# Tokens' rows scattered into expert order, in place of a table of slots

## The chip, the cores and the metric

The kernel runs on one core of one Trainium2 chip. The metric is the device time of one execution in microseconds: the median of several runs. Before the change it is 4458.95 us (three runs, 4456.1 to 4466.6).

## The reference

Three layers, one after the other, on 8 batches of 3072 tokens with 256 columns, in float32:

```python
# 1. spectral layer, for each batch
X = np.fft.rfft(x, axis=1)                                   # over the 3072 tokens
Yr = Xr @ w_r - Xi @ w_i + b_r;  Yi = Xr @ w_i + Xi @ w_r + b_i
Yr = sign(Yr) * max(|Yr| - 0.01, 0)                          # the same for Yi
y = irfft(Yr + 1j * Yi, n=3072, axis=1).reshape(24576, 256)
# 2. mixture of 8 experts, the best one for each token
logits = normalized(y) @ normalized(expert_emb).T / tau
e = argmax(logits);  gate = softmax(logits)[e]
z = gate * (max(y @ w1[e], 0) @ w2[e])                       # 256 -> 1024 -> 256
# 3. dense MLP, 256 -> 2048 -> 256
h = z @ w_in;  out = max(0.01 * h, h) @ w_out                # its weights come in float64
```

## The kernel before

Each product runs as three products of rounded parts (high by high, high by low, low by high), so an eviction from PSUM is a pair: ScalarE copies the high part, VectorE subtracts for the low part (`split_evict`, L165). The order of all work is written out by hand; each engine works in that order, and waits where an operand or a buffer is not ready.

**Spectral layer.** A batch runs through a main stage (`main_step`, L797, steps g = 0 to 25) and a second half (the loop at L868, 37 steps `n2`). The transform over 3072 tokens is one over 96 and one over 32. `s1` (L464) is the first transform over 96; it reads the input tile `xt`, two buffers of 16 rows of 96 tokens, which hold one batch together, loaded in 8 quarters (`load_x`, L355). `mix` (L484) multiplies with the weights, `s2` and `s2i` go over 32 and back. In the second half `swap` (L539) transposes, and `s1i` (L595) makes the last transform over 96: its `ev1` copies the result from PSUM to `yr` (VectorE, L605), `ev2` sums squares (ScalarE, L609), and every second row SP stores two of them to `y1` in DRAM (L613); `yr` has three buffers. In the same steps `s1` already runs for the next batch, whose input tile is thereby read row by row. The last three steps of a second half run together with the first three of the next main stage (`MERGE`).

Beside this, `split_job` (L449) prepares the experts' weights, 128 pieces in all: SP loads one, ScalarE rounds it, GpSimd subtracts, SP stores both parts to DRAM; its tile `hl` has two buffers. It runs in three of four main steps, from step 10 of batch 0 on.

**Routing.** `routing(b)` (L619) gives a list of 22 small steps, most of them on VectorE, that compute each token's expert, gate and slot. Its slots are in regions, one for each expert. The steps are popped from `todo` in the next batch's main stage, one a step, two in every fourth (L815). Then 32 scatters follow (L651), popped from `scat` one a step in that batch's second half (L892): for 96 tokens each, GpSimd writes the token's number, 4 bytes, to its slot in `permd`, the inverse permutation, by an indirect DMA. `block_list` (L692) computes which blocks of 256 slots run, which expert's weights each needs, and gathers the blocks' rows of `permd`, which TensorE turns into the index columns `pidx`. It runs twice: for the 65 blocks surely full after six batches, and for the rest.

**Experts.** `experts` (L193) runs 103 blocks of 256 rows, 8 steps each: `gather_x` fetches the block's rows of `y1` by two indirect DMAs on GpSimd, `trans` transposes them, `mm1` and, a block later, `mm2` multiply; `send` evicts and scatters the rows to `y2` by token (GpSimd, L268). Weights are loaded by SP, addressed by a register. The first blocks run inside the last batch's second half, one step every two, and beside its routing and scatters. Each step also runs one step of `decoder` (L1057), which brings the MLP's weights from float64.

**MLP.** `mlp` (L935) runs 48 tiles of 512 tokens. `load` (L948) fetches a tile of `y2` by a plain transfer on SP, three tiles ahead; before the first one, 24 matmuls on `pw` run (L1041).

Of the kernel before, what the change touches and what calls it, by code (L numbers as in the profile page):

```python
# [1 line left out]

# [8 lines left out]
F32 = mybir.dt.float32  # L11
F32R = mybir.dt.float32r
BF16 = mybir.dt.bfloat16
I32 = mybir.dt.int32
# [14 lines left out]
REG = T // BLK  # L29
NROW = E * REG + E - 1  # L30
# full blocks of the tokens of all batches but two; the rest
# [3 lines left out]
# three runs take turns, with a set of weights each; a run goes through its part of the second list  # L35
# backwards, so that it begins there with the expert that its part of the first ended with
# [3 lines left out]
# a batch's second half: buffers of the swapped rows, steps from the swap to the last transform, and  # L40
# the steps that the next batch's first ones run with
# [17 lines left out]
def constants():  # L59
# [75 lines left out]
    li[:, NA + 1:] = T * np.arange(E)  # L135
# [6 lines left out]
def build(ctx: ExitStack, tc: tile.TileContext, a: dict, out: bass.AP):  # L142
# [6 lines left out]
    permd = dram.tile([NROW * BLK, 1], I32, name="permd")  # L149
    gated = dram.tile([T], F32, name="gated")  # L150
    y1 = dram.tile([T + 1, D], F32, name="y1")
    y2 = dram.tile([T, D], F32, name="y2")
# [9 lines left out]
    pidx = keep.tile([128, 2, NBLK], I32, name="pidx")  # L162
    dummy = keep.tile([1, 1], F32, name="dummy")

# [28 lines left out]
    def experts(st, big, extra):  # L193
        """Yields after each step."""
        def pool(name, bufs):
            return st.enter_context(tc.tile_pool(name=name, bufs=bufs, side="right", reuse_waits="tile"))
        wp, xp, tp, hp, op = pool("ew", 1), pool("ex", 3), pool("et", 2), pool("eh", 10), pool("eo", 4)
        W1, W2 = big
        for s in (1, 2):
            W1.append(wp.tile([128, 4096], F32R, name=f"W1_{s}"))  # L200
            W2.append(wp.tile([128, 4096], F32R, name=f"W2_{s}"))
# [6 lines left out]
        def gather_x(b):  # L208
            if b >= NBLK:
                return  # L210
            i = lidx(b)
            t = xp.tile([128, 2, D], F32R, tag="xg", name="xg")
            for h in range(2):
                nc.gpsimd.indirect_dma_start(
                    out=t[:, h, :].bitcast(F32), out_offset=None, in_=y1[0:TA, :] if b < NA else y1,
                    in_offset=IndirectOffsetOnAxis(ap=pidx[:, h, i:i + 1], axis=0))
            xg[b] = t

# [42 lines left out]
        def send(b, t, p):  # L261
            i = lidx(b)
            o = op.tile([128, D], F32, tag="o", name="eo")
            if t == 0:
                nc.scalar.activation(o, p, AF.Copy)  # L265
            else:
                nc.vector.tensor_copy(o, p)
            ins = nc.gpsimd.indirect_dma_start(  # L268
                out=y2, out_offset=IndirectOffsetOnAxis(ap=pidx[:, t, i:i + 1], axis=0),
                in_=o, in_offset=None, bounds_check=T - 1, oob_is_err=False)  # L270
            nc.gpsimd.memset(dummy, 0.0)
            no_dep(ins, "y2", "every token is written once")

        def finish(b):
            p = O.pop(b)
            for t in range(2):
                send(b, t, p[:, t, :])

        def last(b):
            """The second product of the last block, one half after the other."""  # L280
            w = W2[b % 3].rearrange("p (s f d) -> p s f d", s=2, f=8)
            for t in range(2):
# [7 lines left out]
                send(b, t, p)  # L290

        gather_x(0)
        gather_x(1)
# [4 lines left out]
        for b in range(NBLK):  # L298
            for f in range(8):
# [4 lines left out]
                if f == 2:  # L304
                    gather_x(b + 2)
# [13 lines left out]
    # ------------------------------------------------------------ spectral layer, routing  # L319
    def spectral(big, expert_start):  # L320
        with ExitStack() as st, ExitStack() as mst:
# [50 lines left out]
            def prologue2(wst):  # L372
                # behind the first loads
# [14 lines left out]
            def prologue3():  # L388
                """What a batch's second half needs; a list of small steps."""
# [5 lines left out]
                w = NROW * BLK // 1280  # L395
                pads = {}

                def fill():
                    """Padding entries of the slot table; the row that they point to."""
                    zrow = rp.tile([1, D], F32, tag="lg", name="zrow")  # L400
                    pad = pads[0] = rp.tile([128, w], I32, tag="inc", name="pad")
                    nc.gpsimd.memset(pad, T)
                    nc.gpsimd.memset(zrow, 0.0)
                    nc.sync.dma_start(y1[T:T + 1, :], zrow)
# [8 lines left out]
                def trans():  # L413
                    """The normalized expert embeddings, transposed."""
# [7 lines left out]
                def init():  # L422
# [4 lines left out]
                slots = permd.rearrange("(p q) o -> p (q o)", p=128)  # L427
# [3 lines left out]
                         trans, init, fill]  # L431
                        + [lambda q=q: nc.sync.dma_start(slots[:, w * q:w * q + w], pads[0]) for q in range(10)])

            # the experts' weights, split into their two parts in DRAM
# [146 lines left out]
            def logits3():  # L581
# [8 lines left out]

                return ev

            cur = {}

            def s1i(b, n2):  # L595
                """Returns the two halves of its eviction."""
# [546 lines left out]
```

## Time and profile before

| what | value |
|---|---|
| median of 3 runs | 4458.95 us (4456.1 to 4466.6) |
| profiled execution, its span | 4538.9 us; the trace holds no time around it |
| TensorE busy | 4309.5 us (95%) |
| VectorE, ScalarE, GpSimd busy | 2305.2, 1848.4, 799.5 us |
| mean granted TensorE clock | 0.966 |
| spectral layer with routing | 0 to 1099 us |
| last routing, experts | to 2332 us |
| MLP | to 4538.9 us |
| indirect DMAs: `permd`, `xg`, `y2` | 256, 206, 206 |

The page cuts the span into 40 slices of 113 us. Busy share in tenths, the granted clock of TensorE in tenths, and GB/s moved:

```
PE   9897777887999999999999999999999999999999
PEclk9898878898999999999999999999999999999999
GB/s 175 121 125 91 99 85 109 112 67 122 38 109 114 95 96 94 235 50 118 149 48 19 29 20 29 19 29 19 29 20 29 19 29 19 29 20 29 20 19 15
```

The first ten slices are the spectral layer; from the eleventh on TensorE is busy nearly all the time. Second halves and main stages are cut below at the first `swap` transpose of a batch (L542) and at its fourth `mix` (L492).

### The profile page before, as it was taken

The page shows a single profiled execution, that of the slowest core. Times are in us where ns is not written, and L with a number is a line of the kernel's source. Part 1 is how long each engine was busy: PE and PEld are TensorE (multiplying, and loading weights), DVE is VectorE, ACT ScalarE, POOL GpSimd, SP SyncE. Part 2 cuts the span into 40 slices and gives each one's busy share as a digit, 9 for nine tenths or more (in the row PEclk, how much of TensorE's full clock was granted, in tenths as well). Part 3 has the DMA queues.
Part 4 walks back from the last instruction along what each step waited for, and adds up shares of the span by engine and source line. Part 5 has one row for each costly group of instructions (what it writes and reads, how often), then busy time and mean ns, then how long its engine had stood idle before and what let it go on. Part 6 is the DMA issues. An engine that isn't in the chain of part 4 may idle for free.

```text
span 4538.9 us, 78688 instructions
## 1 busy us (share of the span) xinstructions
PE 4309.5 (95%) x30288; PEld 3982.4 (88%) x30288; DVE 2305.2 (51%) x4836; ACT 1848.4 (41%) x4172; POOL 799.5 (18%) x1298
## 2 busy tenths in 40 slices
PE   9897777887999999999999999999999999999999
PEld 8776666776899999999998999998999999999898
DVE  5665555674345555543344444444444444444453
ACT  4454443443233333333344444444444444444443
POOL 1323334304533333333310000000000000000000
PEclk9898878898999999999999999999999999999999
DMA  6443333326133222613410000000000000000000
GB/s 175 121 125 91 99 85 109 112 67 122 38 109 114 95 96 94 235 50 118 149 48 19 29 20 29 19 29 19 29 20 29 19 29 19 29 20 29 20 19 15
DMA packets 136458, 305.14 MB, mean 67 GB/s; under 512 B 27716, under 2 KB 80444, under 8 KB 131732
## 3 DMA queue, kind: packets, MB, share of 16 engines
q1 hardware_dynamic: 105236, 241.27, 17.1%
q0 software_dynamic: 30848, 58.85, 4.3%
q8 instruction: 239, 3.92, 0.4%
q14 instruction: 135, 1.11, 0.1%
HBM read 542.30 MB, written 111.88 MB: 144 GB/s over the span
## 4 chain that ended last, share of the span: by engine, by line
PE 89%; issue 5%; another core or an unknown queue 3%; DMA 1%; POOL 1%; DVE 1%; ACT 1%; SPq 0%; POOLq 0%; ACTq 0%; DVEq 0%
PE mpH L979 24%; PE mpO L1004 24%; PE pH L242 13%; PE pO L258 13%; PE pu L492 5%; PE py L514 2%; PE ps L470 2%; PE pyo L578 2%; PE pz L530 1%; PE pv L542 1%; PE pT L226 1%; PE mpT L964 1%; PE mpl L1031 0%; POOL permd L655 0%
## 5 line engine op out<-in xcount | busy, mean ns | idle before, releaser
L1004 PE MATMUL mpO<-W,mgh 128*128 128x256 f32 x6016 | 1103.4, 281 | 0.0
L979 PE MATMUL mpH<-mxh,W 128*128 128x512 f32 x3072 | 1087.2, 395 | 0.3 <-ACT mxh L166 0.3
L985 DVE TENSOR_TENSOR mg<-mpH,ms 128x512 f32<-128x512 f32 x768 | 530.8, 691 | 1091.0 <-ACT ms L984 1089.8
L1004 PEld LDWEIGHTS mpO<-W,mgh 128*128 128x128 f32 x6016 | 965.3, 188 | 61.7
L984 ACT ACTIVATE ms<-mpH 128x512 f32<-128x512 f32 x768 | 459.2, 598 | 1234.4 <-PE mpH L979 1231.8
L1004 PE MATMUL mpO<-W,mgl 128*128 128x256 f32 x3008 | 842.0, 280 | 0.0
L242 PE MATMUL pH<-xh,W 128*128 128x256 f32 x3296 | 734.0, 285 | 8.9 <-ACT xh L166 4.8
L246 DVE SCALAR_TENSOR_TENSOR ehl<-pH,ehh 128x256 fp32r<-128x256 f32 x824 | 346.9, 423 | 646.7 <-ACT ehh L245 549.7
L979 PEld LDWEIGHTS mpH<-mxh,W 128*128 128x128 f32 x3072 | 575.1, 187 | 107.4 <-ACT mxh L166 0.5
L258 PE MATMUL pO<-W,ehh 128*128 128x256 f32 x3264 | 632.3, 286 | 4.6 <-issue 2.7
L245 ACT ACTIVATE ehh<-pH 128x256 fp32r<-128x256 f32 x824 | 310.1, 383 | 791.4 <-PE pH L242 763.1
L979 PE MATMUL mpH<-mxl,W 128*128 128x512 f32 x1536 | 605.4, 394 | 0.2 <-DVE mxl L167 0.2
L242 PEld LDWEIGHTS pH<-xh,W 128*128 128x128 f32 x3296 | 576.7, 193 | 12.7 <-issue 5.4
L1004 PEld LDWEIGHTS mpO<-W,mgl 128*128 128x128 f32 x3008 | 565.8, 188 | 0.0
L994 DVE TENSOR_TENSOR mgl<-mg,mgh 128x512 fp32r<-128x512 f32 x768 | 522.6, 680 | 0.0
L258 PEld LDWEIGHTS pO<-W,ehh 128*128 128x128 f32 x3264 | 508.9, 192 | 5.5 <-issue 5.5
L993 ACT ACTIVATE mgh<-mg 128x512 fp32r<-128x512 f32 x768 | 480.2, 625 | 0.0
L242 PE MATMUL pH<-xl,W 128*128 128x256 f32 x1648 | 468.8, 284 | 2.3 <-issue 2.1
L258 PE MATMUL pO<-W,ehl 128*128 128x256 f32 x1632 | 462.9, 284 | 2.1 <-issue 2.1
L268 POOL DMA_INDIRECT y<-eo,pidx x206 | 207.5, 1007 | 730.4 <-ACT eo L265 695.5
L242 PEld LDWEIGHTS pH<-xl,W 128*128 128x128 f32 x1648 | 318.5, 193 | 3.4 <-issue 3.4
L979 PEld LDWEIGHTS mpH<-mxl,W 128*128 128x128 f32 x1536 | 287.9, 187 | 36.7 <-DVE mxl L167 0.5
(192 smaller groups left out, 5520.8 us busy)
## 6 DMA issues: line engine op xcount, KB each, us to landing
W<-w1d SPq DMA_DIRECT2D x101, 2048.0 KB
W<-w2d SPq DMA_DIRECT2D x101, 2048.0 KB
xt<-in_x_dram SPq DMA_DIRECT2D x64, 384.0 KB
y<-yr SPq DMA_DIRECT2D x128, 192.0 KB
mxr<-y SPq DMA_DIRECT2D x47, 512.0 KB
out_dram<-mo SPq DMA_DIRECT2D x47, 512.0 KB
wf<-in_moe_w_dram SPq DMA_DIRECT2D x128, 128.0 KB
w1d<-hl SPq DMA_DIRECT2D x64, 256.0 KB
```

Of the source, the lines that this page charges most:

```text
L242: nc.tensor.matmul(p, l, r, start=(i == 0), stop=(i == 5))
L245: nc.scalar.activation(hh, p, AF.Relu)
L246: nc.vector.scalar_tensor_tensor(hl, p, 0.0, hh, op0=ALU.max, op1=ALU.subtract)
L258: nc.tensor.matmul(O[b][:, t, :], l, r, start=(f == 0 and i == 0 and t == 0), stop=(f == 7 and i == 2 and t == 1))
L268: ins = nc.gpsimd.indirect_dma_start(out=y2, out_offset=IndirectOffsetOnAxis(ap=pidx[:, t, i:i + 1], axis=0), in_=o, in_offset=None, bound ...
L492: nc.tensor.matmul(p, l, r, start=(i == 0), stop=(i == 5))
L979: nc.tensor.matmul(p, l, r, start=(j == 0), stop=(j == 5))
L984: nc.scalar.activation(s, p, AF.Copy, scale=0.01)
L985: nc.vector.tensor_tensor(g, p, s, op=ALU.max)
L993: nc.scalar.activation(gh, g, AF.Copy)
L994: nc.vector.tensor_tensor(gl, g, gh, op=ALU.subtract)
L1004: nc.tensor.matmul(O[i][t // 2][:, t % 2, :], l, r, start=(f == 0 and j == 0 and t % 2 == 0), stop=(f == 15 and j == 2 and t % 2 == 1))
```

## The change

The table of slots goes, and with it `y1`, `y2` and `pidx`. New DRAM tensors: `xs`, the rows in slot order (regions of 97 blocks for each expert, and 7 blocks of padding), `ys`, the experts' results in the order of the blocks, and `slotd`, each token's slot.

- The last transform's rows are not stored to `y1`: they are copied into the next batch's input tile, in the place of the row that `s1` has read (for the last batch into a tile of their own, `y7`).
- When the slots are known, GpSimd scatters these rows of 1 KB to `xs`, two scatters in each main step of the next batch after step 10, and one in each step of its second half until none is left. Only then is the input tile loaded for the batch after: in main steps 21 to 24 and steps 4 to 7 of the second half, a quarter each.
- `todo` is popped three times a main step; weight splitting runs in steps 4 and later of batch 0, and in steps 3 to 13 of the others, two pieces in odd steps.
- `block_list` gathers nothing; it gives the blocks' first rows `wrow`, which SP reads into a register, and the tables `thr`, `off` and `dlt`, by which `places` computes where a token's result lies, in 35 small VectorE steps behind the decoder's. The first list runs a batch earlier.
- A block of the experts is one plain load from `xs` and one plain store to `ys`, both on SP. Behind the last slots of each expert zeros are scattered (`pad`); the padding blocks are written at the start from a tile of zeros.
- The MLP loads a tile by four indirect gathers on GpSimd from `ys`.

Its core:

```diff
-        def gather_x(b):
+        def load_x(b):
             i = lidx(b)
+            r = nc.sync.value_load(wrow[0:1, i:i + 1], min_val=0, max_val=(NROW - 1) * BLK)
             t = xp.tile([128, 2, D], F32R, tag="xg", name="xg")
-            for h in range(2):
-                nc.gpsimd.indirect_dma_start(
-                    out=t[:, h, :].bitcast(F32), out_offset=None, in_=y1[0:TA, :] if b < NA else y1,
-                    in_offset=IndirectOffsetOnAxis(ap=pidx[:, h, i:i + 1], axis=0))
+            nc.sync.dma_start(t.bitcast(F32), xs[bass.ds(r, BLK), :].rearrange("(p h) d -> p h d", h=2))
...
         def finish(b):
             p = O.pop(b)
-            for t in range(2):
-                send(b, t, p[:, t, :])
+            o = op.tile([128, 2, D], F32, tag="o", name="eo")
+            nc.scalar.activation(o[:, 0], p[:, 0], AF.Copy)
+            nc.vector.tensor_copy(o[:, 1], p[:, 1])
+            nc.sync.dma_start(result(b), o)
...
+            def row(b, n2):
+                if b == B - 1:
+                    return y7[0][:N1, n2, :]
+                return xt[b + 1, n2 // 4][:, n2 % 4, :]
...
                 def ev1():
-                    nc.vector.tensor_copy(yr[:, n2 % 2, :], p)
+                    nc.vector.tensor_copy(yr, p)
...
-                    if n2 % 2 == 1:
-                        r0 = b * S
-                        nc.sync.dma_start(
-                            y1[r0:r0 + S, :].rearrange("(p r) d -> p r d", r=N2)[:, n2 - 1:n2 + 1, :],
-                            yr)
...
                 def scatter(n2):
-                    if n2 == 0:
-                        nc.gpsimd.iota(tok, pattern=[[1, N2]], base=b * S, channel_multiplier=N2)
                     nc.gpsimd.memset(dummy, 0.0)
                     ins = nc.gpsimd.indirect_dma_start(
-                        out=permd, out_offset=IndirectOffsetOnAxis(ap=si[:, n2:n2 + 1], axis=0),
-                        in_=tok[:, n2:n2 + 1], in_offset=None)
-                    no_dep(ins, "perm", "every slot is used once")
+                        out=xs, out_offset=IndirectOffsetOnAxis(ap=si[:, n2:n2 + 1], axis=0),
+                        in_=row(b, n2), in_offset=None)
+                    no_dep(ins, "in", "every slot is used once")
...
                 if g >= 3:
-                    for _ in range(2 if last else 1 + (g % 4 == 3)):
+                    for _ in range(3):
                         if todo:
                             todo.pop(0)()
...
-                if g % 4 < 3 and (b or g > 9):
+                if g > 10:
+                    for _ in range(2):
+                        scatter()
+                if g >= 4 if b == 0 else 3 <= g < 14:
                     split_job()
-                if not last and g % 3 == 1 and g // 3 < 8:
-                    load_x(b + 1, g // 3)
+                    if b and g % 2:
+                        split_job()
+                if b == 0 and g % 3 == 1 and g // 3 < 8:
+                    load_x(1, g // 3)
+                if b and g in (21, 22, 23, 24):
+                    refill(b + 1, g - 21)
...
+            nc.gpsimd.dma_start(
+                xs[E * REG * BLK:, :].rearrange("(n p) d -> p n d", p=128),
+                warm.bitcast(F32)[:, None, :].to_broadcast([128, 2 * (E - 1), D]))
...
+                    scatter()
+                    if b and n2 in (4, 5, 6, 7):
+                        refill(b + 1, n2)
...
             def load(i):
-                n = 2 if i == 0 else 4
-                for t in range(0, 4, n):
-                    nc.sync.dma_start(xr[i][:, t:t + n].bitcast(F32), y2v[:, 4 * i + t:4 * i + t + n, :])
+                for t in range(4):
+                    nc.gpsimd.indirect_dma_start(
+                        out=xr[i][:, t].bitcast(F32), out_offset=None, in_=ys,
+                        in_offset=IndirectOffsetOnAxis(ap=slot[:, 4 * i + t:4 * i + t + 1], axis=0))
```

`refill(b, q)` is `load_x` of the spectral layer where there is such a batch; behind the last one it loads the first block's expert weights. In the experts' pools `eh` goes from 10 to 9 buffers and `eo` from 4 of 256 columns to 2 of 512.

## Rows read from the trace of the kernel before

**Rows 1.** Windows, experts and MLP: stretch and us; each engine's busy time; clock, DMA, GB/s.

```profile
1325.00:2335.00 1010.00, 1010.00 (x8494) 1009.36 (x8493) 484.57 (x1261) 338.45 (x876) 351.27 (x508) 1.00 0.33 113
2335.00:4538.90 2203.90, 2199.06 (x14219) 1979.78 (x14217) 1085.16 (x1728) 941.44 (x1728) 0.00 (x0) 1.00 0.07 24
```

**Rows 2.** Windows, second halves of batches 1 to 6: first, last, sum. Engines: PE, PEld, DVE, ACT, POOL.

```profile
194.80:273.80 79.00, 49.38 (x345) 42.47 (x345) 32.70 (x87) 33.08 (x117) 34.36 (x69) 0.74 0.22 51
...
885.40:960.80 75.40, 49.62 (x345) 42.80 (x345) 32.93 (x87) 32.06 (x114) 24.30 (x49) 0.75 0.15 40
sum 467.80, PE 299.26 PEld 262.29 DVE 198.02 ACT 198.29 POOL 195.68; mean PE 49.88 PEld 43.71 DVE 33.00 ACT 33.05 POOL 32.61
```

**Rows 3.** Windows: second half 0, mains 1 and 7, second half 7, last scatters.

```profile
95.50:136.30 40.80, 40.51 (x346) 37.07 (x346) 32.68 (x89) 33.30 (x117) 2.51 (x4) 1.00 0.35 102
136.30:194.80 58.50, 58.10 (x375) 52.18 (x374) 48.10 (x113) 28.40 (x60) 13.03 (x17) 1.00 0.60 173
960.80:1019.70 58.90, 57.37 (x359) 50.62 (x357) 48.92 (x140) 23.54 (x41) 1.41 (x2) 1.00 0.20 77
1019.70:1099.40 79.70, 48.23 (x294) 40.73 (x295) 27.82 (x75) 26.99 (x99) 39.32 (x73) 0.72 0.72 125
1138.00:1253.00 115.00, 105.02 (x809) 100.50 (x809) 34.13 (x80) 29.94 (x80) 64.68 (x111) 0.97 0.18 37
```

**Rows 4.** Timeline of VectorE, batch 1's second half: start, us, instruction, [idle before <-releaser].

```profile
203.67 0.41 DVE L545 TENSOR_TENSOR vl<-pv,vh 96x256 fp32r<-96x256 f32 x1
215.25 0.42 DVE L605 COPY yr<-pyo 96x256 f32<-96x256 f32 x1 [11.17 <-remote]
```

**Rows 5.** Timeline of TensorE in the same stretch.

```profile
205.41 1.01 PE L470 MATMUL ps<-f,xt 96*128 96x96 f32 x4
216.62 0.63 PE L542 MATMUL pv<-ident,Z 128*96 128x128 f32 x2 [10.20 <-issue]
```

**Rows 6.** Timeline of GpSimd in the same stretch; nine more scatters lie between.

```profile
203.60 0.91 POOL L655 DMA_INDIRECT permd<-tok,si  x1 [0.22 <-issue]
...
216.36 0.91 POOL L655 DMA_INDIRECT permd<-tok,si  x1 [0.83 <-DMA permd<-tok,si]
```

**Rows 7.** Waits of the whole run: waiter <- waited for: total us, times, longest.

```profile
DVE yr L605 <- remote: 130.0, 16, 13.1
...
POOL permd L655 <- DMA permd<-tok,si: 42.1, 27, 4.5
```

**Rows 8.** Windows: the start, the loads of constants, plain steps of main stage 0.

```profile
0.00:22.00 22.00, 17.01 (x115) 14.07 (x116) 7.39 (x14) 7.59 (x14) 3.71 (x11) 0.93 0.82 204
20.00:48.00 28.00, 27.00 (x137) 24.03 (x137) 14.83 (x34) 9.93 (x19) 11.14 (x21) 0.78 1.15 302
...
67.90:95.40 27.50, 27.25 (x180) 24.51 (x179) 19.18 (x45) 11.97 (x25) 6.22 (x8) 1.00 0.67 193
```

**Rows 9.** Instructions on tile `hl`: ns min/median/max, first and last start.

```profile
L458 ACT ACTIVATE hl<-wf x128: 400/408/419, 66.1 to 874.5; 128x256 fp32r<-128x256 f32 x128
L459 POOL TENSOR_TENSOR hl<-wf,hl x128: 724/742/904, 66.6 to 875.0; 128x256 fp32r<-128x256 f32 x128
L460 SPq DMA_DIRECT2D w1d<-hl x64: 545/546/1353, 67.5 to 851.9; - x64
```

**Rows 10.** Timeline of ScalarE: a splitting copy that waits for its buffer.

```profile
167.55 0.42 ACT L458 ACTIVATE hl<-wf 128x256 fp32r<-128x256 f32 x1 [0.74 <-DMA w1d<-hl]
```

**Rows 11.** Timeline of SP: the store whose landing that copy awaited.

```profile
164.52 0.55 SPq L460 DMA_DIRECT2D w1d<-hl  x1
```

**Rows 12.** Timeline of GpSimd: the last scatter of the experts.

```profile
2332.61 0.98 POOL L268 DMA_INDIRECT y<-eo,pidx  x1 [1.81 <-DVE eo L267]
```

**Rows 13.** Timeline of SP: the first loads of the MLP.

```profile
2335.08 1.77 SPq L954 DMA_DIRECT2D mxr<-y  x4
```

**Rows 14.** Instructions of line L684, VectorE, in routing: ns min/median/max.

```profile
L684 DVE TENSOR_TENSOR ex<-ex,ob x8: 411/958/965, 176.2 to 1132.7; 96x256 f32<-96x256 f32 x8
```

**Rows 15.** Instructions of line L1092, VectorE, in the experts' stage.

```profile
L1092 DVE TENSOR_TENSOR e<-e,p x32: 412/415/417, 1342.6 to 1986.6; 128x256 f32<-128x256 f32 x32
```

More of the change, by code (lines that the diff above doesn't have):

```diff
@@ L1 @@
 from contextlib import ExitStack
+from itertools import chain
 import numpy as np
@@ L259, in mm2 @@
                                      stop=(f == 7 and i == 2 and t == 1))
[L261 to L272, printed above, removed]
         def finish(b):
             p = O.pop(b)
-            for t in range(2):
-                send(b, t, p[:, t, :])
+            o = op.tile([128, 2, D], F32, tag="o", name="eo")
+            nc.scalar.activation(o[:, 0], p[:, 0], AF.Copy)
+            nc.vector.tensor_copy(o[:, 1], p[:, 1])
+            nc.sync.dma_start(result(b), o)
         def last(b):
             w = W2[b % 3].rearrange("p (s f d) -> p s f d", s=2, f=8)
+            o = op.tile([128, 2, D], F32, tag="o", name="eo")
             for t in range(2):
@@ L430, in prologue3 @@
                          dma(trif, a["tri"]), dma(scan, a["scan"]), dma(eord, a["eord"]), dma(li, a["li"]),
[L431 to L432 removed]
+                         trans, init])
             jobs = []
@@ L690, in routing, with pad, index, scatter @@
                 return steps, sc
+            def pad():
+                zero = rp.tile([128, D], F32, tag="ex", name="zero")
+                zi = rp.tile([128, E, 2], I32, tag="zi", name="zi")
+                co = rp.tile([128, E], F32, tag="co", name="zco")
+                v = nc.vector
+                def index():
+                    v.memset(zero, 0.0)
+                    v.tensor_tensor(co, carry, li[:, NA + 1:], op=ALU.add)
+                    v.tensor_scalar(co, co, li[:, NA:NA + 1], None, op0=ALU.add)
+                    v.tensor_copy(zi[:, :, 0], co)
+                    v.tensor_scalar(zi[:, :, 1], co, 128.0, None, op0=ALU.add)
+                def scatter(e, h):
+                    nc.gpsimd.memset(dummy, 0.0)
+                    ins = nc.gpsimd.indirect_dma_start(
+                        out=xs, out_offset=IndirectOffsetOnAxis(ap=zi[:, e, h:h + 1], axis=0),
+                        in_=zero, in_offset=None)
+                    no_dep(ins, "in", "rows behind the last slot")
+                return [index] + [lambda e=e, h=h: scatter(e, h) for e in range(E) for h in range(2)]
             def block_list(last):
@@ L896, in spectral @@
                         next(ex)
-                assert not scat and not squares
+                assert not squares
                 if last:
@@ L932, in spectral, with places, mlp @@
             return ex
-    def mlp(W):
+    def places(wp, row):
+        slot, s, t = (wp.tile([128, 256], I32, tag=t, name=t + "p").bitcast(F32)[:, :T // 128] for t in "ept")
+        yield lambda: nc.sync.dma_start(slot, slotd.rearrange("(p t) -> p t", p=128))
+        yield lambda: nc.vector.tensor_copy(s, slot)
+        for j in range(2 * E):
+            c = slice(j, j + 1)
+            yield lambda: nc.vector.tensor_scalar(t, slot, thr.rearrange("p e l -> p (e l)")[:, c], dlt[:, c],
+                                                  op0=ALU.is_ge, op1=ALU.mult)
+            yield lambda: nc.vector.tensor_tensor(s, s, t, op=ALU.add)
+        yield lambda: nc.vector.tensor_copy(row, s)
+    def mlp(W, slot):
         with ExitStack() as st:
@@ L1108, in build @@
             W = ml.tile([128, 16384], F32R, name="W")
-            steps = decoder(ml, W)
+            row = ml.tile([128, T // 128], I32, name="row")
+            steps = chain(decoder(ml, W), places(ml, row))
             for _ in ex:
```

155 lines of the change are left out of this document (76 added, 79 removed).

## The prediction

> **What bounds the kernel now.** I cut the span by stage first. In the two long stages at the end, 1325 to 2335 us (experts) and 2335 to 4538.9 us (MLP), TensorE is busy 1010.0 of 1010.0 us and 2199.1 of 2203.9 us at clock 1.00 [rows 1]: nothing that only moves data can shorten them. What can be won or lost lies in the first 1325 us.
>
> There the batches' second halves stand out. Batch 0's takes 40.8 us with TensorE busy 40.5 at clock 1.00; those of batches 1 to 6 run the same 344 to 346 matmul records in 75 to 81 us each, 467.8 us in all, at clocks of 0.70 to 0.76 [rows 2, 3]. Batch 7's, which has expert steps in it, takes 79.7 us at clock 0.72. The main stages between (23 steps of some 2.55 us) are healthy: 58.1 of 58.5 us busy at 1.00 [rows 3].
>
> The difference is the permutation scatter. GpSimd issues one 4-byte-per-row scatter per step, and in a burst they follow at about 1.2 us each. Some 8 us into a burst everything else stops: VectorE finishes at 204.08 and its next row copy starts at 215.25 after 11.17 us idle, for an event that the profile cannot name; TensorE finds 10.20 us idle [rows 4, 5]. GpSimd itself walks on, until it too waits for one of its own scatters to land [rows 6]. Over the run the row copies lose 130.0 us that way and the scatters 42.1 us on their own landings [rows 7]. Batch 0's second half has no scatters and no stall. The 32 scatters of the last batch, spread over 115 us, leave TensorE 105.0 us busy at clock 0.97 [rows 3]. So a dense burst of 4-byte DRAM writes costs a second half 37 us: idle TensorE, and the 1.2 GHz clock level after it.
>
> The profiled span, 4538.9 us, is 80 us above the median of 4458.95. Since the last 3214 us sit on TensorE at full clock, these 80 us must be in the stalls, which the recording lengthens; I sum against 4538.9 and say below why the result stands for the median too.
>
> **The change part by part.**
>
> *Second halves, batches 1 to 6.* The y1 store and its three buffers go; the row copy writes into the input tile of the next batch, whose row TensorE read some five steps earlier. The scatters move to main stages; two of 32 stay. Each should become batch 0's: 467.8 - 6 x 40.8 = 223 us gained [rows 2, 3]. Ends: nothing gained if the stall follows the scatters, 223 if it is theirs alone. I take 223, because a burst of 1 KB rows is a different load: from 20 to 48 us GpSimd's queue and SP's moved 302 GB/s in packets of 0.4 to 4 KB and TensorE was busy 27.0 of 28.0 us [rows 8], and the experts' stage fetches and sends 1 KB rows by indirect transfers with no idle TensorE [rows 1]. What is late next there is the input tile: its second half loads in steps 4 to 7, after the last scatters landed, for a transform at step 12, eight steps or 9 us later; a load of this kind needs 3 to 4 us at the quarter-tile rate of [rows 8] (384 KB at 204 GB/s is 1.9 us, queued up to four deep). Hidden; without that cover some 3 us a batch.
>
> *Second half of batch 7.* Its matmuls are stretched like the others': 48.2 us busy there, and 49.9 in the mean of batches 1 to 6 against 40.5 unstalled [rows 2, 3], so 48.2 x 40.5/49.9 = 39 us. The first expert block now waits in SP's queue for the scatters issued so far, as its rows are addressed by a register; TensorE wants it five steps in. I add 4 us and some slack: 44 us, a gain of 36. Ends: 0 and 40.
>
> *Startup and batch 0.* A padding write of 1792 rows, 1.8 MB, joins the first input loads, when the DMA engines are 0.82 busy at 204 GB/s [rows 8]: 9.0 us if the loads queue behind it, 0 if it slips between. Weight splitting starts at step 4 instead of 10, one job a step. I take +6, range 0 to 13.
>
> *Main stages, batches 1 to 6.* Three things are squeezed. (a) The weight-splitting jobs, 17 a batch over 23 steps, go into steps 3 to 13, three per two steps. A job holds one of two `hl` buffers from ScalarE's copy to its store's landing: 0.41 + 0.74 + 0.55 us [rows 9] and the landing, which the wait at 167.55 puts 2.5 us after its store's issue ended at 165.07 [rows 10, 11]: 4.2 us, so two buffers pass a job each 2.1 us. 17 jobs want 35.7 us, the 11 steps have 28. ScalarE waits in order, with the next `uh` eviction that TensorE needs behind it; by my estimate some 2.5 us of that is absorbed at the two ends, 5 us is not. (b) Routing's 22 steps come three a main step instead of 1.25. VectorE is 0.70 busy in plain steps [rows 8], so 40.8 of main 1's 48.1 us [rows 3] are base and 7 to 8 are routing; squeezed into 8 steps (20.4 us) it wants 22, and it also collides with splitting (below). It shares (a)'s steps, so I count only the larger. (c) From step 11 GpSimd does two scatters a step, 2.4 us of 2.55, and in steps 11 to 13 five splitting ops of 0.74 us wait behind them, with ScalarE's buffers: +3. Together +8 a batch, 48 us; ends 0 and 20 each. After step 13 nothing on GpSimd is waited for until the input tile is refilled.
>
> *Main stage 7.* Four jobs are left and routing is squeezed the same way: +3 (0 to 5).
>
> *Block lists, gather of slots, eh 10 to 9, eo 4 to 2.* The lists lose a gather and gain some small vector steps in the middle of TensorE's full stage; a ninth `hh` frees with the product before it. 35 vector steps for the MLP's places run as extra expert steps. 0, hidden behind the 1010 us of TensorE [rows 1]; without cover 10 us.
>
> *Experts to MLP.* Before: a 0.98 us scatter at 2332.61, landed by 2335.08 when SP loads [rows 12, 13]. Now a store on SP (0.55 + 2.5 as above, so +0.6), and then four gathers at 1.2 us where two loads stood, 3.7 us until the fourth is issued. +4, ends 2 and 7. In the MLP 192 gathers of 1 us lie beside 2204 us.
>
> Sum: 4538.9 - 223 - 36 + 6 + 48 + 3 + 4 = 4341 us. This holds for the median: once the stalls are gone no stretch is left in which the recording could cost 80 us, so the median gains 80 us less, 118 us (2.6%).
>
> **One rule weighed.** Next to splitting, VectorE's two-input multiply of routing takes 958 ns in most batches and 411 at least; next to indirect transfers two-input ops stay at 417 ns at most [rows 14, 15]. The Trainium skill ("SBUF — State Buffer", section "SBUF: two separate sides") says that such a VectorE op and a GpSimd op share one port pair as an exclusive lock, each waiting out the other's whole instruction. The trace agrees for splitting and not for descriptor writing. If indirect transfers also locked it, each of 15 steps in 7 main stages would give VectorE 1.8 + 0.9 = 2.7 us against 2.55, some 20 us.
>
> **Rivals.**
> - *The stall moves with the scatters* (the other side). Were the cause GpSimd's dense issue, whatever is written, the burst of 30 scatters at 1.2 us would stop the main stages 1 to 7 as it stops second halves now. For it: the rate is the same, and the queue is the same. Against: [rows 8], and the experts' 1 KB rows. The change loses as soon as more than two thirds of the median's stall survives, since then what is left of 179 us falls under the 61 us of costs. Wholly moved: 4459 + 61 = 4520 us.
> - *Half the stall survives*, for instance as late landings that hold the input tile: half of the median's 259 - 80 = 179 us, so 4341 + 90 = 4431.
> - *The squeezed main stages cost more*: (a), (b) and (c) add up instead of overlapping, 20 us a batch: 4341 + 72 = 4413. For it: ScalarE, VectorE and GpSimd are all near full in the same steps.
> - *They cost nothing*, as the slack between engines is larger than I think: 4341 - 51 = 4290.
> - *The lock holds for row scatters too*: 4341 + 20 = 4361.
>
> **How the numbers follow.** The forecast 4341, own range 4300 to 4385, has 0.56. The stall moves 0.13; half survives 0.08; main stages cost more 0.15; they cost nothing 0.05 (and a little below); the lock 0.03. The range of 8 in 10 reaches from 4285 to 4425; left out are the first rival and most of the second. A measurement tells 0.2% (9 us) here. Faster takes all cases but the first: 0.85; the same, where losses just balance, 0.02; slower 0.13.
>
> **What would show it.** Right: second halves 1 to 6 near 41 us at clock 1.00; no wait of VectorE's row copy for an unnamed event; scatter bursts from main step 11 with TensorE busy beside them; ScalarE waiting in line L458's successor for stores of `hl` in steps 3 to 13; profiled span and median within some 20 us. Wrong: a main stage of 80 us or more with clock under 0.8, or PE gaps of 10 us inside a burst. A second half of 50 us with gaps at step 12 would say that the refill is late.

## The result, and the profile after

The changed kernel takes 4343.3 us (median of four runs, 4339.2 to 4345.5); the kernel before, run beside it, 4462.8 (4456.1 to 4469.9). The ratio is 0.973, with a 95% interval of 0.9716 to 0.9744: 119.5 us gained, where 118 were forecast. The profiled execution after has a span of 4337.4 us.

The windows of the changed kernel, cut at the same marks as [rows 1 to 3] (stretch, us, then busy time of PE, PEld, DVE, ACT, POOL, and clock, DMA share, GB/s). In order: second halves of batches 0, 1 and 6, with the sum of all seven; main stages 1 and 3, with the sum of 1 to 6; main stage 7 and second half 7.

```profile
96.10:136.90 40.80, 40.55 (x344) 36.99 (x345) 32.49 (x87) 32.30 (x115) 0.73 (x1) 1.00 0.08 24
204.00:244.70 40.70, 40.42 (x344) 36.98 (x345) 32.59 (x87) 32.28 (x114) 4.17 (x9) 1.00 0.21 56
...
750.30:791.10 40.80, 40.51 (x346) 37.04 (x346) 32.66 (x89) 32.35 (x114) 4.08 (x9) 1.00 0.23 55
sum 285.10, PE 283.24 PEld 258.98 DVE 228.26 ACT 226.25 POOL 26.63; mean PE 40.46 PEld 37.00 DVE 32.61 ACT 32.32 POOL 3.80
...
136.90:204.00 67.10, 62.30 (x375) 52.78 (x373) 49.72 (x113) 28.31 (x59) 41.46 (x73) 1.00 0.54 162
...
354.10:423.60 69.50, 63.30 (x376) 52.76 (x374) 49.31 (x113) 29.71 (x60) 41.38 (x73) 1.00 0.53 156
...
sum 409.90, PE 376.93 PEld 317.62 DVE 302.77 ACT 176.81 POOL 248.64; mean PE 62.82 PEld 52.94 DVE 50.46 ACT 29.47 POOL 41.44
...
791.10:852.40 61.30, 57.99 (x355) 50.27 (x354) 47.19 (x111) 25.25 (x47) 33.66 (x64) 1.00 0.36 111
852.40:893.80 41.40, 36.14 (x295) 32.65 (x296) 26.70 (x75) 26.52 (x100) 3.71 (x8) 0.96 0.69 254
```

The stall is gone: a second half with the next batch's transform in it takes 40.7 us at clock 1.00, where [rows 2] show 79.0 and 75.4 at 0.74 and 0.75. The main stages, GpSimd busy in them for 41 us in place of 13, became 6 to 10 us longer; TensorE is idle 5 to 6 us in each, and the rest is in longer busy time.

Behind the spectral layer the stage of the experts, from the last `swap` to the last product, and that of the MLP have to be cut at the same marks in both kernels. Before:

```profile
1099.40:2331.90 1232.50, 1222.52 (x10217) 1217.63 (x10216) 568.80 (x1486) 410.51 (x1068) 453.64 (x674) 1.00 0.31 106
2339.50:4538.90 2199.40, 2195.53 (x14200) 1977.30 (x14200) 1085.11 (x1728) 940.77 (x1727) 0.00 (x0) 1.00 0.07 23
```

After:

```profile
893.80:2106.90 1213.10, 1213.10 (x10216) 1212.78 (x10214) 589.35 (x1529) 418.15 (x1068) 48.76 (x95) 1.00 0.32 113
2118.20:4337.40 2219.20, 2215.79 (x14200) 2004.71 (x14200) 1085.30 (x1728) 940.44 (x1727) 182.06 (x186) 1.00 0.07 23
```

So the whole difference of the two spans, 201.5 us, comes apart like this; it is larger than the 119.5 us of the timed runs because the profiled execution before is 80 us longer than those (see "The median" below). The main stages 1 to 6 of the kernel before run from 58.5 to 61.9 us:

```profile
sum 356.70, PE 350.16 PEld 313.39 DVE 289.20 ACT 177.29 POOL 85.44; mean PE 58.36 PEld 52.23 DVE 48.20 ACT 29.55 POOL 14.24
```

| stretch | before | after | measured | forecast |
|---|---|---|---|---|
| up to main stage 1 | 136.3 | 136.9 | +0.6 | +6 |
| main stages 1 to 6 | 356.7 | 409.9 | +53.2 | +48 |
| second halves 1 to 6 | 467.8 | 244.3 | -223.5 | -223 |
| main stage 7 | 58.9 | 61.3 | +2.4 | +3 |
| second half 7 | 79.7 | 41.4 | -38.3 | -36 |
| experts | 1232.5 | 1213.1 | -19.4 | 0 |
| experts to MLP | 7.6 | 11.3 | +3.7 | +4 |
| MLP | 2199.4 | 2219.2 | +19.8 | 0 |

Two terms of 19 to 20 us were put at nothing, and cancel.

The waits of the changed kernel (total us, times, longest) that answer to [rows 7] and to the forecast of main-stage costs:

```profile
ACT hl L449 <- DMA w2d<-hl: 62.7, 38, 3.3
...
ACT hl L449 <- DMA w1d<-hl: 56.0, 40, 2.8
...
DVE xt L602 <- PE pyo L569: 22.2, 28, 1.4
```

The row copy (now into `xt`) waits for its own product and for nothing unnamed; 130.0 us of [rows 7] are gone. New are the 118.7 us in which ScalarE's splitting copy waits for stores of `hl`. In the kernel before they were 4.9 and 1.1:

```profile
ACT hl L458 <- DMA w1d<-hl: 4.9, 5, 2.8
```

### The profile page after: what moved, and what is told of

Read it like the earlier page. It is cut to its first block, busy times and chain, and to the rows that moved or that the text cites. A ratio compares the mean times of both kernels' runs of the same rounds, so it can differ in the third digit from the quotient of the medians.

```text
span 4337.4 us, 78356 instructions
## 1 busy us (share of the span) xinstructions
PE 4280.0 (99%) x30286; PEld 3960.8 (91%) x30286; DVE 2335.4 (54%) x4880; ACT 1855.3 (43%) x4172; POOL 578.6 (13%) x893
## 4 chain that ended last, share of the span: by engine, by line
PE 83%; issue 7%; POOL 5%; DMA 3%; DVE 1%; ACT 1%; SPq 0%; ACTq 0%; POOLq 0%
PE mpO L1041 25%; PE mpH L1016 25%; PE pO L267 14%; PE pH L251 14%; POOL xs L642 4%; PE pu L483 1%; DMA w2d<-hl 1%; DMA w1d<-hl 1%; POOL hl L450 1%; PE pT L235 1%; PE mpT L1001 1%; PE py L505 1%; PE mpl L1068 1%; PE ps L461 0%; PE pz L521 0%
## 5 line engine op out<-in xcount | busy, mean ns | idle before, releaser
L1041 PE MATMUL mpO<-W,mgh 128*128 128x256 f32 x6016 | 1123.6, 283 | 0.0
L1041 PEld LDWEIGHTS mpO<-W,mgh 128*128 128x128 f32 x6016 | 976.9, 188 | 61.2
L1041 PE MATMUL mpO<-W,mgl 128*128 128x256 f32 x3008 | 853.6, 284 | 0.0
L989 POOL DMA_INDIRECT mxr<-ys,row x192 | 187.9, 979 | 2865.8 <-PE mpT L1001 1772.9
```

Of the source, the lines that this page charges most:

```text
L989: nc.gpsimd.indirect_dma_start(out=xr[i][:, t].bitcast(F32), out_offset=None, in_=ys, in_offset=IndirectOffsetOnAxis(ap=slot[:, 4 * i + t: ...
L1041: nc.tensor.matmul(O[i][t // 2][:, t % 2, :], l, r, start=(f == 0 and j == 0 and t % 2 == 0), stop=(f == 15 and j == 2 and t % 2 == 1))
```

## The experiments

Three groups: what makes the stall, what the squeezed main stages cost, and whether the difference between chips belongs to the kernel. They ran in three sessions on three chips, where the kernel before showed 4557.6, 4454.4 and 4445.0 us (medians of three, seven and three runs).

**No scatters at all.** The kernel before, with its 256 scatters gone. Not in the diff below: as the table of slots then holds padding alone, the blocks gather other rows, the experts' sends drop out, and the MLP reads `y1`.

```diff
...
-                sc = [lambda n=n: scatter(n) for n in range(N2)]
+                sc = [lambda: None for n in range(N2)]
...
```

> The kernel before without its permutation scatters (left out: the 256 scatters of 4 bytes; the blocks take other rows, the sends of rows drop out by their bound or land elsewhere, the MLP reads y1). All else, the y1 stores of the second halves too, stays. Theory (the burst of 4-byte writes stops the engines): second halves 1 to 7 become like batch 0's, 41 us at clock 1.00, no wait of the row copy for an unnamed event; time about 4463 - 179 = 4284 us, and the profiled span within 20 us of it, as nothing is left that the recording lengthens. Rival (the second half stalls by itself, through the y1 stores and row copies that share it): second halves stay over 70 us, time above 4430 us. In between: the difference to 4284 is what the stores cost.

Measured: 4251.6 us, beside 4557.6 for the kernel before, ratio 0.933 (0.930 to 0.936). The sums of its second halves 1 to 6 and of its main stages 1 to 6:

```profile
sum 244.30, PE 242.80 PEld 222.09 DVE 195.77 ACT 198.25 POOL 12.12; mean PE 40.47 PEld 37.01 DVE 32.63 ACT 33.04 POOL 2.02
...
sum 352.00, PE 349.64 PEld 313.62 DVE 289.60 ACT 177.29 POOL 77.54; mean PE 58.27 PEld 52.27 DVE 48.27 ACT 29.55 POOL 12.92
```

With the y1 stores still there the second halves are 244.3 us, to a tenth what the change reached: the stores cost nothing, the scatters all of it. The time came out 32 us lower than expected. The 179 us of the expectation counted the second halves alone; the profiles of the kernel before and of this one also differ by 19.1 us in the experts' stage, where the last batch's scatters run, and by 4.7 in main stages 1 to 6. The window of that stage, TensorE busy throughout, where the kernel before took 1232.5 us:

```profile
830.10:2043.50 1213.40, 1213.40 (x10217) 1213.03 (x10216) 565.90 (x1486) 409.42 (x1068) 421.61 (x609) 1.00 0.32 88
```

On this chip all that the scatters cost is 4557.6 - 4251.6 = 306 us.

**The scatters alone moved.** The kernel before, its 4-byte scatters in the next main stage.

```diff
-                    for _ in range(2 if last else 1 + (g % 4 == 3)):
+                    for _ in range(3):
...
+                if g > 10:
+                    for _ in range(2):
+                        if scat:
+                            scat.pop(0)()
...
```

> The kernel before with one thing of the change alone: its 4-byte scatters go into the next batch's main stage, two in each step after step 10, with routing three steps at a time ahead of them. Theory (the 4-byte burst stalls whatever stands beside it): the stall moves with the scatters, main stages 1 to 6 grow to 85 to 100 us with gaps of TensorE near 10 us and clock under 0.85, second halves shrink to 41; time within 50 us of the kernel before, 4415 to 4515. Rival (the stall needs the scatters and the y1 stores of the second half together): no gap in the main stages, over 100 us faster, about 4320.

Measured: 4483.2 us, ratio 0.984 (0.979 to 0.989). Windows of its main stage and second half 3, and TensorE's longest gap there (start, us, instruction, idle before it):

```profile
388.60:475.00 86.40, 67.21 (x375) 57.70 (x373) 47.83 (x113) 29.73 (x62) 40.45 (x74) 0.88 0.65 122
...
475.00:521.70 46.70, 43.95 (x344) 40.06 (x345) 32.81 (x87) 33.20 (x117) 7.00 (x13) 0.93 0.34 85
```

```profile
467.42 0.58 PE L514 MATMUL py<-uh,g2h 128*128 128x256 f32 x1 [8.54 <-ACT uh L166]
```

The stall went with the scatters: the main stage 86.4 us at clock 0.88 with a gap of 8.5 us, the second half, in which GpSimd still has 7.0 us of work, 46.7 where 41 was expected. 232 us above the kernel without scatters remain of 306, so moving them is worth 74 us in this kernel, more than the 50 I gave as a limit. Most of the stall stays as long as 4 bytes are written; the next runs change that alone.

**The changed kernel, writing 4 bytes of each row.** First into a dense table as before, which the diff below shows; then at the row's own place, 1 KB apart. In both the experts' blocks load other rows.

```diff
-                        out=xs, out_offset=IndirectOffsetOnAxis(ap=si[:, n2:n2 + 1], axis=0),
-                        in_=row(b, n2), in_offset=None)
+                        out=permd, out_offset=IndirectOffsetOnAxis(ap=si[:, n2:n2 + 1], axis=0),
+                        in_=row(b, n2)[:, 0:1], in_offset=None)
...
```

> The changed kernel with its 256 row scatters writing 4 bytes of each row into a dense table, as the kernel before did (left out: the other 1020 bytes; the experts' blocks take other rows). Same issue, same steps, same indices. Theory (what is written decides): gaps near 10 us come into main stages 1 to 7, their clock falls under 0.85, each grows by 20 to 37 us; time 4343 + 7 x 24 = 4510 us (range 4460 to 4600), profiled span above the median by 30 us or more. Rival (GpSimd's issue at that rate, or the second half, made the stall): no change, 4335 to 4350.

> The changed kernel with its row scatters writing 4 bytes of each row, at the row's own place in xs, so 1 KB apart (left out: the rest of each row; the experts' blocks take other rows). If the size of a write decides: as with the dense table, 4510 us (4460 to 4600) with gaps near 10 us in the main stages. If it is neighbours in the same dense table that decide (several writes into one stretch of memory): no gaps, 4335 to 4350 us.

Measured: 4613.4 us (ratio 1.012, 1.009 to 1.016) and 4602.5 (1.010, 1.007 to 1.013). Main stage 1, its second half and main stage 3 of the kernel with 4 bytes at 1 KB:

```profile
137.50:234.10 96.60, 65.91 (x375) 54.94 (x373) 49.33 (x113) 28.20 (x59) 44.91 (x81) 0.86 0.37 103
234.10:274.90 40.80, 40.51 (x346) 37.07 (x346) 32.69 (x89) 32.38 (x114) 0.00 (x0) 1.00 0.01 2
412.30:511.10 98.80, 68.66 (x375) 56.23 (x374) 48.23 (x113) 29.52 (x60) 44.80 (x81) 0.86 0.35 101
```

The timelines of its VectorE, TensorE and GpSimd around 197 us:

```profile
197.65 0.69 DVE L174 TENSOR_TENSOR ul<-pu,uh 128x512 fp32r<-128x512 f32 x1 [12.10 <-issue]
```

```profile
197.67 0.58 PE L506 MATMUL py<-uh,g2h 128*128 128x256 f32 x1 [9.96 <-issue]
```

```profile
195.97 0.91 POOL L643 DMA_INDIRECT xs<-xt,si  x1 [0.21 <-issue]
...
197.19 0.92 POOL L643 DMA_INDIRECT xs<-xt,si  x1 [0.22 <-issue]
...
198.41 0.91 POOL L643 DMA_INDIRECT xs<-xt,si  x1 [0.22 <-issue]
```

This is the picture of [rows 4 to 6] in another place: VectorE and TensorE stand for 12.1 and 10.0 us while GpSimd issues a scatter every 1.2 us. The issue, the steps and the count of the scatters are those of the changed kernel, which has no such gap; in these stages only the bytes of each transfer, and the scale of the index, differ. That refutes the rival in which the rate of issue stalls, and as both places give the same, neighbours in a table are not it either. Each transfer also reads only 4 bytes; whether the read or the write matters no run separates, and "write" stands here for both.

Both times lie above the 4510 that was expected, and above its range to 4600. Main stages 1 and 3 grew by 29.5 and 29.3 us where 24 was taken, main stage 7 by 33.9, and the last batch's scatters, which were not counted, stall the experts: in 153.8 us there TensorE is busy 124.6 at clock 0.88. Beside the kernel before (4557.6) these kernels are 1.0 to 1.2% slower, so the new place of the scatters does not by itself explain the gain.

**64, 256 and 512 bytes.** The second of these kernels, with more of each row; the diff has 64 bytes against 4.

```diff
-                        out=xs.rearrange("n (k w) -> (n k) w", w=1),
+                        out=xs.rearrange("n (k w) -> (n k) w", w=16),
...
-                        in_=row(b, n2)[:, 0:1], in_offset=None)
+                        in_=row(b, n2)[:, 0:16], in_offset=None)
...
```

> The changed kernel with its row scatters writing 64 bytes of each row, at the row's place (left out: the rest of each row; the experts' blocks take other rows). With 4 bytes main stages 1 to 7 grew to 95 to 99 us from 61 to 69, at clock 0.84 to 0.88, and the time to 4602; with 1024 bytes there is no gap. If the cost is one per write, whatever lies below a full row: as with 4 bytes, main stages 90 us and more, 4500 to 4610 by how hard this chip stalls. If the cost comes from a write of a few bytes alone, 4330 to 4345, main stages near 68.

> The same with 256 bytes of each row. If the stall fades with size: main stages between the two, 70 to 85 us, 4360 to 4450. If it goes at one size below this: near 68 us, 4340. If it goes only above: as with 4 bytes. The Trainium skill (DMA: Bandwidth & Descriptors, Specifications) puts a read-modify-write under every transfer of less than 512 bytes; were that the cause, 64 and 256 bytes would both stall as 4 bytes do, 4500 to 4610.

> The same with 512 bytes of each row. Theory (small writes alone stop the engines): no gap in main stages 1 to 7, 68 us each at clock 1.00, and 4325 to 4345 us, as with whole rows. Rival (whole rows are free for another reason than their size, for instance as they are one stretch of memory): gaps as with 4 bytes, 4500 and above.

Measured: 4334.3, 4337.0 and 4334.8 us, beside 4445.0 for the kernel before; ratios 0.9747, 0.9753 and 0.9748, with intervals of 0.003 to both sides. Main stage 3 with 64 bytes, and its second half 7; then main stage 3 with 512 bytes:

```profile
354.20:423.80 69.60, 63.40 (x375) 52.78 (x373) 49.03 (x113) 29.71 (x60) 41.43 (x73) 1.00 0.42 120
...
853.10:887.70 34.60, 33.83 (x294) 30.99 (x295) 26.61 (x75) 26.25 (x99) 4.29 (x10) 1.00 0.81 295
```

```profile
356.10:425.50 69.40, 63.21 (x375) 52.74 (x373) 48.82 (x113) 29.65 (x60) 41.42 (x73) 1.00 0.47 138
```

With 64 bytes the main stage is that of whole rows, 69.6 against 69.5 us. So the stall is a matter of writes of a few bytes, with its limit somewhere between 4 and 64. The Trainium skill (DMA: Bandwidth & Descriptors, Specifications) has a read-modify-write under every transfer below 512 bytes. No trace here shows that, and it is not what stops the engines: main stage 3 differs by 0.2 us between 64 and 512 bytes. These runs were on a chip with a smaller stall than the 4-byte ones, and the changed kernel with 4 bytes was not run there; but there too the kernel before stands 4445.0 - 4251.6 = 193 us above the time without scatters (an estimate, as that time is from the other chip), and these show nothing of it. They also price one wait: where the first blocks do not wait for scattered rows, second half 7 takes 34.6 us, so that wait and the weights queued behind it cost 41.4 - 34.6 = 6.8.

**The main stages.** Three edits of the changed kernel, run with it on one chip: four `hl` buffers; splitting one job a step from step 9, its subtraction on VectorE beyond step 10; and the same with routing at two and three steps in turn and the scatters one step later (its diff is against the second).

```diff
-                    hl = m2.tile([128, 2, 256], F32R, tag="hl", name="hl")
+                    hl = m2.tile([128, 2, 256], F32R, tag="hl", name="hl", bufs=4)
```

> The changed kernel with four buffers for hl, the tile of the weight splitting, in place of two. If the buffers' landings set the pace of steps 3 to 13 of main stages 1 to 6 (my step (a): 35.7 us wanted, 28 there), about 5 us a batch goes: 4343 - 30 = 4313 us, and ScalarE no longer waits for stores of hl. If routing's VectorE work (step (b)) fills the same time anyway, 4335 to 4345. As main stage 7, which has no splitting but routing, still grew by 2.4 us and stages 1 to 6 by 9, I expect about half: 4325.

```diff
...
-                if g >= 4 if b == 0 else 3 <= g < 14:
-                    split_job()
-                    if b and g % 2:
-                        split_job()
+                if g >= 4 if b == 0 else g >= 9:
+                    split_job(nc.vector if b and g > 10 else nc.gpsimd)
```

> The changed kernel with the weight splitting of batches 1 to 6 moved to one job a step from main step 9 on, where routing is done, and with the subtraction on VectorE beyond step 10, where GpSimd scatters. This removes (a) and (c) and leaves (b): main stages 1 to 6 come to main stage 7's 61.3 us from 68.3, so 4343 - 6 x 6.5 = 4304 us. If VectorE, with 0.42 us more a step, or ScalarE has no room there, 4320 or above.

```diff
-                    for _ in range(3):
+                    for _ in range(2 + g % 2):
...
-                if g > 10:
+                if g > 11:
```

> As the kernel with moved splitting, and with routing popped two and three steps in turn in place of three, the scatters from step 12 on. This takes (b) as well: main stages 1 to 6 near 59.5 us, main stage 7 near 59.5: 4304 - 7 x 1.5 = 4294 us. If the squeeze of routing costs nothing beyond what splitting does, as for moved splitting alone; if the later scatters hold the input tile's refill, second halves grow by 3 us each and it is slower than that, 4320.

> The changed kernel as it is, once more, beside the kernel before on the same chip. The kernel before took 4456 to 4470 us in one session and 4551 to 4563 in another, with profiled spans 2 us under the times. Theory (the size of the stall differs from chip to chip or session to session, and the changed kernel has none): 4335 to 4350 us whatever the kernel before shows beside it, so that the gain is 2.7% to 4.7% by where it is measured. Rival (some chips are slower in all they do): 4343 us only if the kernel before shows about 4463, some 4430 if it shows 4557.

Measured on that chip: before 4454.4; the changed kernel 4340.4 (4339.4 to 4342.1), ratio 0.9746 (0.973 to 0.976); four buffers 4318.5 (4317.3 to 4320.1), 0.9696 (0.968 to 0.971); moved splitting 4307.0 (4303.6 to 4313.1), 0.9675 (0.966 to 0.969); both 4303.4 (4297.7 to 4307.3), 0.9661 (0.964 to 0.968). The sums of main stages 1 to 6, one kernel each in that order:

```profile
sum 388.80, PE 365.59 PEld 315.89 DVE 302.65 ACT 178.97 POOL 246.21; mean PE 60.93 PEld 52.65 DVE 50.44 ACT 29.83 POOL 41.03
```

```profile
sum 371.20, PE 358.50 PEld 317.13 DVE 312.93 ACT 178.68 POOL 196.42; mean PE 59.75 PEld 52.86 DVE 52.15 ACT 29.78 POOL 32.74
```

```profile
sum 367.80, PE 357.64 PEld 317.94 DVE 313.22 ACT 178.74 POOL 183.36; mean PE 59.61 PEld 52.99 DVE 52.20 ACT 29.79 POOL 30.56
```

From the changed kernel's 409.9 two more buffers take 21 us, moving the splitting 39, the slower routing with later scatters 3 more; 352.0 is what such stages take in the kernel without scatters, so 15.8 us are left that no run takes apart. Of the 39 the time shows 33; the second halves, where the moved splitting now ends, take back 5. With four buffers no wait of the splitting copy for a store is left; what it waits for is its own loads:

```profile
ACT hl L449 <- DMA wf<-in_moe_w_dram: 45.8, 37, 3.3
```

I had priced four buffers at "about half", 18 us under the changed kernel, and step (a) alone at 30; they gave 21.9 under the one run beside them. Routing's share was overpriced: 3.6 us between the last two kernels, whose runs overlap, where I expected 10. The last kernel is 37 us below the changed one, with runs that do not overlap. It has two `hl` buffers; four of them with the moved splitting were not run.

**The changed kernel again**, on the third chip.

> The changed kernel unchanged once more, beside the kernel before on the chip of this call. The kernel before has shown 4454, 4463 and 4558 us. If chips differ only in the stall, this shows 4335 to 4345 whatever the kernel before shows beside it. If a chip is slower in all, it moves with it, to 4430 beside 4558.

Measured: 4341.9 us, beside 4445.0; ratio 0.9764 (0.974 to 0.979). In the three sessions in which it ran the changed kernel shows 4343.3, 4340.4 and 4341.9, the kernel before 4462.8, 4454.4 and 4445.0. It was not run on the chip that shows 4557.6.

## Why the prediction was right, and where it was not

*The stall (right, and shown).* Forecast: theirs alone, 223 us. Without scatters the second halves are 244.3 us, with row scatters elsewhere 244.3 too. That a burst of 1 KB rows is a different load was argued from [rows 8]; the runs with 4 and 64 bytes show it, at the same issue, steps and count.

*The rivals.* That the stall moves is false for rows, and true for 4-byte writes (main stages of 96 to 99 us). The lock is not seen either (its price, 7 x 15 x 0.15 us, comes to 16 and not to 20). In the second part of main stage 4, where GpSimd only scatters, the window of the changed kernel is

```profile
512.00:530.00 18.00, 17.86 (x118) 16.08 (x118) 12.92 (x30) 6.36 (x11) 15.18 (x29) 1.00 0.59 166
484.00:510.00 26.00, 22.22 (x126) 17.92 (x125) 17.22 (x40) 9.98 (x22) 16.07 (x29) 1.00 0.65 198
```

GpSimd is in scatters for 15.2 of 18.0 us and TensorE busy 17.9. VectorE's operation with both inputs in SBUF takes there, and then in batch 0's main stage, where there are no scatters:

```profile
L510 DVE TENSOR_TENSOR z<-z,t 128x256 f32<-128x256 f32 x7 | 3.0, 426 | 0.2
```

```profile
L510 DVE TENSOR_TENSOR z<-z,t 128x256 f32<-128x256 f32 x11 | 4.7, 425 | 0.4
```

The loss is in the other window, the steps with splitting and routing: 3.8 of 26 us idle.

*Main stages 1 to 6 (right size, one part mis-weighed).* Forecast +48, measured +53.2. Step (a), the two buffers, is shown by the timeline of ScalarE and by four buffers, 21 us or 3.5 a batch where 5 was worked out:

```profile
499.87 0.42 ACT L449 ACTIVATE hl<-wf 128x256 fp32r<-128x256 f32 x1 [2.26 <-DMA w1d<-hl]
```

Step (c), GpSimd's splitting behind scatters, is within the 18 us (388.8 - 371.2, 2.9 a batch, +3 forecast) that moving the splitting gives beyond four buffers; the other effects of moving it are in that too. I had let (b) hide under (a); it is worth 0.6 us a batch in the profiles, the later scatters included, and in the times it is not clear of noise. Together that is 7.0 of the 8.9 us a batch; the rest, which the last kernel still has over the kernel before, is not traced to a cause.

*Second half 7 (right size, by two errors that offset) and main stage 7 (right).* 41.4 against 44, 61.3 against 61.9. For second half 7 I took 39 us of matmuls and 4 of waiting, with some slack; with 64 bytes, where the first blocks wait for no scattered rows, it takes 34.6, and the wait is worth 6.8.

*Startup (mis-sized).* +6 forecast, 0.6 measured. The first 22 us move 268 GB/s, where the kernel before moved 204, with TensorE busy 16.3 us in place of 17.0; so the padding write seems to slip between the loads, as in my lower end.

*Experts (missed).* I had seen in [rows 3] that the last batch's scatters leave TensorE idle 10 us, and costed their going at nothing. The stage is 19.4 us shorter, and in the changed kernel TensorE is busy 1213.1 of 1213.1 us. 10 us of the gain are idle time; the other 9 are busy time (1222.5 against 1213.1 us for the same records), with which the clock of 0.97 in [rows 3] goes. The kernel before without its scatters shows the same stage at 1213.4 us, so the 19 us go with them; where none of them run, both kernels keep the same pace (8494 matmul records in 1010.0 us [rows 1], 8343 in 992.0 in the changed kernel). The step that failed is that the sum ended the stall with batch 7's second half.

*MLP (missed, cause open).* I costed the 192 gathers at nothing beside TensorE, and the stage became 19.8 us longer. Little of that is the start: at the hand-off TensorE waits for one gather after the other, and its clock falls; the kernel before crossed it in 7.6 us at clock 1.00. One of these waits, then the windows of the hand-off and of what follows in the changed kernel:

```profile
2115.87 0.37 PE L1001 MATMUL mpT<-identr,mxr 128*128 128x128 f32 x1 [0.94 <-DMA mxr<-ys,row]
```

```profile
2106.90:2118.20 11.30, 7.37 (x33) 5.32 (x32) 0.46 (x2) 0.66 (x2) 5.86 (x7) 0.86 0.28 78
2118.20:2130.00 11.80, 11.80 (x43) 9.18 (x44) 7.67 (x12) 6.64 (x12) 9.36 (x9) 0.84 0.35 99
```

At 0.84 over 11.8 us that is 2 us. The rest is spread evenly: the `mpO` matmuls take 283 and 284 ns, at any time of the stage. The groups of TensorE's matmuls in the last 200 us of the kernel after, then in the same part of the one before:

```profile
L1041 PE MATMUL mpO<-W,mgh 128*128 128x256 f32 x504 | 94.0, 283 | 0.0
...
L1041 PE MATMUL mpO<-W,mgl 128*128 128x256 f32 x252 | 71.6, 284 | 0.0
```

```profile
L1004 PE MATMUL mpO<-W,mgh 128*128 128x256 f32 x514 | 94.2, 281 | 0.0
...
L1004 PE MATMUL mpO<-W,mgl 128*128 128x256 f32 x258 | 72.2, 280 | 0.0
```

Over the whole stage these two groups are busy 1123.6 and 853.6 us against 1103.4 and 842.0, 32 us more, though neighbouring matmuls overlap in the records. From one step's first `mpH` matmul to the next step's the trace has 2813 ns before and 2840 after (medians), and over 750 such intervals 2143.7 and 2161.8 us: there are the missing 18. GpSimd's last gather starts at 4115.5 and its busy time in these last 200 us is 0, so the gathers that run beside are not the cause. The step goes with the program and not with the chip or the scatters: 2813 ns in both variants of the kernel before, 2840 in the changed kernel with 4 or 64 bytes, four buffers or moved splitting. What in the program it is, the place of the tiles in on-chip memory, the order of TensorE's stream or something else, no run here separates.

*The median (right number, wrong reason).* I put the 80 us between profile and median down to the recording. That step failed. In every later run the time is some 2 us above the span, in stalled kernels too: with dense 4-byte writes the profiled run took 4612.8 us and the other 4613.9. What differs is the size of the stall from session to session, and with them the chips: 4445, 4454, 4463 and 4558 us for the same kernel, while the kernel after stays within 3 us in three of the four. Second halves without scatters take 40.7 us on the chip with the large stall as elsewhere. So the profiled execution before (4538.9) was by all signs one with a large stall, and the timed runs had a smaller one; taking 80 us off the gain gave the right figure by luck, and so did the two terms of 19.4 and 19.8 us, which cancel. The gain is 2.4 to 2.7% where it was measured, and where the kernel before takes 4558 it should be larger, by an estimate 4558 - 4342 = 216 us or 4.7%, which was not run.

## What to carry to other kernels

When VectorE and TensorE stop together with an unnamed releaser while GpSimd walks on, look at what is being written to DRAM. Here moving a burst of 4-byte scatters moved most of its stall with it, while 64 bytes or more per write took it away, and whole rows, which cost the main stages no more than 64 bytes, spare the experts' gather as well. When work is moved into a full stage, count how long its buffers are held against the steps that it is given: two more buffers were worth 22 us here, and a spread over more steps, without them, 37. And sum a forecast against a stage table that covers the whole span; two terms of 20 us that cancel look like none.

## What was not expected of the hardware

- 4 bytes per row stall and 64 do not: main stages of 96.6 to 98.8 us against 67.3 to 69.6, at the same number of writes and the same issue. Why a write of 4 bytes stops engines that do not wait for it the traces do not show.
- The size of the stall goes with the chip or the session: 4445 to 4558 us for one kernel, with its runs in one session within 14 us.
- The MLP's `mpO` matmuls are 2 to 4 ns longer in the kernel after, also where nothing runs on GpSimd, and a step of 18 matmuls takes 2840 ns in place of 2813.
